# Loads paced by attention ticks, a machine model with DMA queue and clock, pair scores in segment 0, and filler matmuls in a fused attention and feed-forward block

## The chip, the cores and the metric

The kernel runs on one core of one Trainium2 chip. The metric is device microseconds (us) of one execution, the median of the runs of a kernel. Every run also has a state: fast, or slow when it is more than 1.5% above the fastest run of the same kernel. "Span" is the time from the first to the last instruction of the one profiled execution; it is about 2 us shorter than the device time. The engines are called TensorE (PE in the profile, its weight loads PEld), VectorE (DVE), ScalarE (ACT), GpSimd (POOL) and SyncE (SP; its DMA issues appear as SPq).

## The reference

It is one block on `x` of 2048 tokens by 640 features, in bf16: layer norm, attention with 32 heads of 20 features, an output projection with a residual, then a second layer norm and a feed-forward part with 1728 hidden features. The attention goes through four segments of 512 tokens. In each, a causal softmax inside the segment is mixed, through a gate, with a linear-attention memory of the earlier segments. Cut to what matters:

```python
h  = x + attn(layernorm(x), wq, wk, wv, wo, beta)
h2 = h + silu(layernorm(h) @ w1) @ w2

# attn, for each segment s of 4 (L = 512 tokens), each of H = 32 heads (Dh = 20):
p     = softmax(qs @ ks.T * Dh**-0.5 + causal_mask)
a_dot = p @ vs
a_mem = (phi(qs) @ M) / (phi(qs) @ z + 1e-6)       # phi(t) = t + 1 if t > 0 else exp(t)
o     = sigmoid(beta) * a_mem + (1 - sigmoid(beta)) * a_dot
M, z  = M + phi(ks).T @ vs, z + sum(phi(ks))
# out = concat(o) @ wo
```

## The kernel before

The Python that builds the kernel does not write instructions in a fixed order. It declares tasks (a matmul group, an exp, a DMA) with a priority, the engines that may run them, an estimated cost and the buffers they need. A list scheduler then plays the tasks through a small model of the machine and emits them in the order that came out. On the chip each engine runs its instructions in exactly that order, with semaphores between the engines. **The model's times never run anywhere, but they decide the order.** This is the part of it that the change touches:

```python
LAT = {PE: 0.125, AC: 0.145, DV: 0.03, PO: 0.07, SP: 0.0}
# ... in schedule(), for each engine that is free, the ready task of lowest priority number:
                        pr = t.prio
                        if e == PE and pemode[0] is not None and t.mode != pemode[0]:
                            pr += 0.02
# ... and then its cost; TensorE always at full speed:
                    if e == SP:
                        engfree[e] = st + 0.06            # SyncE is free again after 0.06 us
                        if t.mode == "tr":                # transposes: a queue of their own
                            b = max(st, xbar[0])
                            xbar[0] = b + t.bw
                            end = b + t.bw + cost
                        else:                             # all other transfers
                            b = max(st, dmaq[0])
                            dmaq[0] = b + t.bw
                            end = b + t.bw + cost
```

All loads come first, whole, on SyncE:

```python
    load_x(0, 1, -100)
    # ... x 1, 2, 3
    load_w("q", wraw[:, 0, :, :], cw(A_wq), -96, 3.4, [(sT0, ["q"])])
    load_w("k", wraw[:, 1, :, :], cw(A_wk), -95, 3.4, [(sT0, ["k"])])
    load_w("wv", wv_sb[:, :, :], cw(A_wv), -94, 3.4)
    # ... beta, x 4-7, wo, x 8-11
    load_w("w1", w1_sb[:, :, :], cw(B_w1), -87, 9.0)
    # ... x 12-15
    dma("w2a", [], [(W["w2"], [0])], lambda e: e.dma_start(out=w2_sb[:, 0:NF - 1, :], ...), -85, 9.0, lane=lane_w2)
    # ... w2b
```

The attention of a segment is eight "ticks" of four heads. A tick has three score tiles (PTA, PTB, PTE). Each takes four of the eight PSUM banks (`sc`), one bank a head; ScalarE then takes the exp, in halves or at once, and GpSimd the causal mask:

```python
            for pi, (pool, pt, js, width, cost) in enumerate((
                    ("PTA", PTA, [(0, 0)], 512, 0.225), ("PTB", PTB, [(1, 0), (3, 384)], 512, 0.23),
                    ("PTE", PTE, [(2, 0)], 256, 0.12))):
                sca = G.alloc("sc", 4)                    # all four score banks: the next tile has to wait
                # ...
                G.task(f"qk{k}{pi}", {PE: cost}, e_qk, [ra], [(sca, [0])], pr - 0.5, mode="r", reserve=[pta])
                halves = [(0, 2), (2, 2)] if width == 512 else [(0, 4)]
                # ... one exp for each half
            # evictions from PSUM may run on either engine:
            G.task(f"oe{k}", {AC: act_c(512) + 0.05, DV: dve_c(512)}, e_ot, ...)
```

The softmax here doesn't subtract the row's maximum and nothing guards it: scores larger than these inputs give would overflow.

Of the kernel before, what the change touches and what calls it, by code (L numbers as in the profile page):

```python
# [22 lines left out]
class _Op:  # L23
    __slots__ = ("eng", "fn", "seq", "waits", "need_inc", "lane", "cnt")

    def __init__(self, eng, fn, seq, lane=None):
        self.eng = eng
        self.fn = fn
        self.seq = seq
        self.waits = []  # L30
        self.need_inc = False
        self.lane = lane
        self.cnt = None

# [9 lines left out]
class Tracker:  # L44


    def __init__(self):
        self.ops = {e: [] for e in ENGS}
        self.K = {e: {} for e in ENGS}
        self.post = {}  # L50
        self.regions = {}
        self.lanes = []

# [23 lines left out]
    def add(self, eng, fn, reads=(), writes=(), order=(), lane=None):  # L77
# [6 lines left out]
        op = _Op(eng, fn, seq, lane=lane)  # L84
        if lane is not None:
            lane.n += 1
            prodkey, pseq = lane, lane.n
        else:
            prodkey, pseq = eng, seq
# [140 lines left out]
LAT = {PE: 0.125, AC: 0.145, DV: 0.03, PO: 0.07, SP: 0.0}  # L230


class Graph:
    def __init__(self, pools):
        self.pools = pools
        self.tasks = []
        self.turns = {}
        self.free_order = ("x", "ps", "ex", "th", "st", "xn", "pK", "rd")
# [42 lines left out]
    def schedule(self):  # L281
# [14 lines left out]
        xbar = [0.0]  # L296
# [48 lines left out]

        now = 0.0
# [5 lines left out]
        while left:  # L352
            progressed = True
            while progressed:
                progressed = False
                for e in ENGS:
# [3 lines left out]
                    for i in cand[e]:  # L360
# [3 lines left out]
                        pr = t.prio  # L364
                        if e == PE and pemode[0] is not None and t.mode != pemode[0]:
                            pr += 0.02
# [4 lines left out]
                        best = ((pr, t.idx), t)  # L371
                    if best is None:
# [14 lines left out]
                    if e == PE:  # L387
                        pemode[0] = t.mode
                    t.start, t.eng = st, e
                    if e == SP:  # L390
                        engfree[e] = st + 0.06
                        if t.mode == "tr":
                            b = max(st, xbar[0])
                            xbar[0] = b + t.bw
                            end = b + t.bw + cost
                        else:
                            b = max(st, dmaq[0])
                            dmaq[0] = b + t.bw
                            end = b + t.bw + cost
# [61 lines left out]

def build(nc, es, A_x, A_wq, A_wk, A_wv, A_wo, A_beta, B_x, B_w1, B_w2, out):
# [53 lines left out]
    mt = sb("mt", [128, 4, 96], F32)  # L516
    wraw = sT[:, :, :].rearrange("p f t -> p (f t)")[:, 0:2 * NC * D].rearrange("p (w c e) -> p w c e", w=2, c=NC)
# [14 lines left out]
    def act_c(n):  # L532
        return 0.00083333 * n + 0.075

    def dve_c(n):
        return n / 960.0 + 0.195
# [10 lines left out]
    def dma(name, reads, writes, fn, prio, bw, mode=None, lat=2.0, lane=None):  # L547
        ln = T.lane(name) if lane is None else lane

        def emit(eng):  # L550
            T.add(SP, lambda e: fn(e), reads=R(*reads), writes=R(*writes), lane=ln)
        return G.task(name, {SP: lat}, emit, reads, writes, prio, mode=mode, bw=bw)
# [9 lines left out]
    def load_x(b0, n, prio):  # L562
        dma(f"x{b0}", [], [(X[b], [0]) for b in range(b0, b0 + n)],
            lambda e: e.dma_start(out=x_tok[:, b0:b0 + n, :], in_=xv[:, b0:b0 + n, :]), prio, 0.68 * n)

    def load_w(k, dst, src, prio, bw, wr=None):
        dma("w_" + k, [], wr or [(W[k], [0])], lambda e: e.dma_start(out=dst, in_=src), prio, bw)

    cw = lambda w: w.rearrange("(c p) e -> p c e", p=128)
    load_x(0, 1, -100)  # L570
    load_x(1, 1, -99)
    load_x(2, 1, -98)
    load_x(3, 1, -97)
    load_w("q", wraw[:, 0, :, :], cw(A_wq), -96, 3.4, [(sT0, ["q"])])
    load_w("k", wraw[:, 1, :, :], cw(A_wk), -95, 3.4, [(sT0, ["k"])])
    load_w("wv", wv_sb[:, :, :], cw(A_wv), -94, 3.4)
    dma("beta", [], [(C, ["beta_bc"])],
        lambda e: e.dma_start(out=beta_bc[:, :],
                              in_=A_beta.rearrange("(o n) -> o n", o=1).to_broadcast([128, H])), -93, 0.3)
    load_x(4, 4, -90)  # L580
    load_w("wo", wo_sb[:, :, :], cw(A_wo), -89, 3.4)
    load_x(8, 4, -88)
    load_w("w1", w1_sb[:, :, :], cw(B_w1), -87, 9.0)
    load_x(12, 4, -86)
    lane_w2 = T.lane("w2")
    dma("w2a", [], [(W["w2"], [0])],
        lambda e: e.dma_start(out=w2_sb[:, 0:NF - 1, :], in_=cw(B_w2[0:(NF - 1) * 128, :])), -85, 9.0, lane=lane_w2)
    dma("w2b", [], [(W["w2"], [1])],
        lambda e: e.dma_start(out=w2_sb[0:64, NF - 1, :], in_=B_w2[(NF - 1) * 128:FF, :]), -84, 0.4, lane=lane_w2)  # L589
# [10 lines left out]
    def vx_alloc(s):  # L600
        VX[s] = G.alloc("Vx")
        return VX[s]

# [70 lines left out]
    rearr("wq", 0, wqr, -40)  # L674
    rearr("wk", 1, wkr, -39)
    WSUB = {"wq": list(range(5)), "wk": list(range(5)), "wv": [0], "wo": [0], "w1": [0], "w2": [0, 1]}


    def layer_norm(tag, b, xa, xsub, dstA, dst, i, prio):
        st = G.alloc("st")  # L680
        xn = G.alloc("xn")

# [9 lines left out]
        G.task(f"{tag}st{b}", {DV: 1.25}, e_stats, [(xa, xsub)], [(st, ["s0", "s1", "mv"])], prio)  # L692
# [9 lines left out]
        def e_apply(eng):  # L702
# [5 lines left out]
        G.task(f"{tag}ap{b}", {DV: 0.48}, e_apply, [(xa, xsub), (st, ["mv", "r"])], [(xn, [0])], prio)  # L708
        dma(f"{tag}tr{b}", [(xn, [0])], [(dstA, [i])],
            lambda e: e.dma_start_transpose(out=dst[:, :, 128 * i:128 * i + 128], in_=xn_rot[:, xn.slot, :]),  # L710
            prio, 0.9, mode="tr", lat=1.8)
# [8 lines left out]
    segs = {}  # L720

    def declare_front(s):

        k0 = 8 * s
        sg = segs[s] = {}
        xTa = G.alloc("xT")
        for i in range(4):
            layer_norm("n1_", 4 * s + i, X[4 * s + i], [0], xTa, xT, i, k0 - 5.0 + 0.6 * i if s else -30 + i)
        vx = vx_alloc(s)
        for i in range(4):  # L730
            ps = G.alloc("ps", 2)
            pr = k0 - 2.2 + 0.4 * i if s else -5 + i
# [24 lines left out]
        for c in range(5):  # L757
            for w in range(2):
                ps = G.alloc("ps", 1)
                pr = k0 - 1.2 + 0.65 * c + 0.3 * w if s else -10 + 0.5 * c + 0.2 * w + (0 if c < 2 else 8)  # L760
# [19 lines left out]
                if phi:  # L780
# [13 lines left out]
                    prp = k0 + 0.3 + 0.5 * c if w == 0 else k0 + 1.0 + 0.8 * c  # L794
                    G.task(f"ph{s}{c}{w}", {DV: 0.75}, e_phi, [(qk[c], [w]), (exa, [0])], [(pa, ["a"])], prp)
# [4 lines left out]
        pr = k0 + 2.6  # L800

        def virt(n, reads, o, i_):
            dma(f"vt{s}{n}", reads, [(qv, [n])], lambda e: e.dma_start(out=o, in_=i_), pr, 0.15, lane=lane_v)  # L803
# [8 lines left out]
    def declare_ticks(s):  # L812
# [3 lines left out]
        ot = G.alloc("otok")  # L816
        sg["ot"] = ot
        for g in range(NG):
# [7 lines left out]
            pts = []  # L826
            for pi, (pool, pt, js, width, cost) in enumerate((
                    ("PTA", PTA, [(0, 0)], 512, 0.225), ("PTB", PTB, [(1, 0), (3, 384)], 512, 0.23),
                    ("PTE", PTE, [(2, 0)], 256, 0.12))):
                sca = G.alloc("sc", 4)  # L830
                pta = G.alloc(pool)
                pts.append(pta)
                pr = k + (0.0, 0.35, 0.7)[pi]

                def e_qk(eng, sca=sca, js=js, qa=qa, ka=ka, ra=ra):
                    fns = []
                    for j, co in js:
                        n = L - 128 * j
                        for r in range(4):
                            fns.append(lambda e, j=j, co=co, n=n, r=r: e.matmul(  # L840
                                sc_all[:, 512 * r + co:512 * r + co + n],
                                lhsT=ka[32 * r:32 * r + DH, 128 * j:128 * j + 128],
                                rhs=qa[32 * r:32 * r + DH, 128 * j:L],
                                start=True, stop=True, tile_position=(32 * r, 0)))
                    T.run(PE, fns, R(ra), R((sca, [0])))
                G.task(f"qk{k}{pi}", {PE: cost}, e_qk, [ra], [(sca, [0])], pr - 0.5, mode="r", reserve=[pta])
                halves = [(0, 2), (2, 2)] if width == 512 else [(0, 4)]
# [307 lines left out]
```

## Time and profile before

| | before |
|---|---|
| device time, median of 2 runs | 447.04 us (446.94 to 447.15) |
| profiled span | 444.3 us |
| mean granted TensorE clock | 0.888 |
| TensorE busy / idle | 325.0 / 119.3 us |
| ScalarE, VectorE, GpSimd busy | 236.0, 205.1, 145.4 us |

The page of the kernel before, its parts 1 and 2. In part 2 each digit is one fortieth of the span (11.1 us), in tenths; PEclk is the granted clock of TensorE.

```profile
PE 325.0 (73%) x2616; PEld 160.0 (36%) x2616; DVE 205.1 (46%) x427; ACT 236.0 (53%) x304; POOL 145.4 (33%) x282
...
PE   0009858785569746865399999999977989665997
...
PEclk9999977987598955599599999999997999885999
```

No engine is full on average, and that average hides stages: three slices in which TensorE does nothing, a stretch in which it is about three quarters busy at a falling clock, a full stretch, and a tail with holes. I cut the span at five events: the first useful matmul, the last exp of segments 0, 1 and 3, and the end. The view of stretches of the kernel before; the columns are the stretch, its length, the busy time of PE, PEld, DVE, ACT and POOL with their instructions, the granted clock, the share of the DMA engines' time, and GB/s:

```profile
0.00:33.40 33.40, 0.00 (x0) 0.00 (x0) 8.65 (x25) 1.63 (x3) 11.47 (x47) 1.00 0.96 319
33.40:120.10 86.70, 63.11 (x496) 29.02 (x496) 47.01 (x121) 59.05 (x77) 34.65 (x72) 0.84 0.21 41
120.10:189.30 69.20, 50.53 (x452) 22.98 (x452) 26.84 (x57) 49.79 (x60) 29.96 (x49) 0.73 0.15 23
189.30:378.30 189.00, 163.48 (x1395) 83.24 (x1395) 98.54 (x182) 116.45 (x150) 64.07 (x103) 0.95 0.17 38
378.30:444.30 66.00, 47.85 (x276) 24.80 (x273) 24.11 (x43) 9.04 (x15) 5.29 (x11) 0.87 0.14 34
```

TensorE is idle for 33.4, 23.6, 18.7, 25.5 and 18.2 us in the five stretches (length less PE busy), and in segments 0 and 1 what it does runs at a clock of 0.84 and 0.73. The timeline of the kernel before says why the first stretch is empty; the columns are start, duration, engine and line, and, in brackets, the idle time before it and what ended it:

```profile
17.35 8.62 SPq L589 DMA_DIRECT2D w_sb<-in_B_w_dram  x1
26.02 10.47 SPq L710 DMA_TRANSPOSE xT<-xn_rot  x4
...
33.43 2.85 PE L738 MATMUL ps_gen<-wv_sb,xT 128*128 128x320 bf16 x10 [33.43 <-DMA xT<-xn_rot]
...
119.04 11.88 SPq L803 DMA_DIRECT2D QKV<-QK  x16
```

The first transpose of the normalised input, which every projection needs, is issued at 26.0 us, after all the loads, and lands at 33.4, behind the bytes still in flight. The last line shows the same at a smaller scale: 16 small copies hold SyncE for 11.9 us, and only then, at 131.0, can it issue the transposes for the output projection. The view of waits of TensorE in the kernel before (us in total, times, longest):

```profile
PE ps_gen L738 <- DMA xT<-xn_rot: 35.6, 2, 33.4
PE ps_sc L840 <- ACT PTB L851: 15.3, 13, 1.9
PE ps_gen L1060 <- DMA hT<-xn_rot: 12.7, 2, 8.8
```

So the big waits are the start, the score matmuls (L840) waiting until the exp has freed the one four-bank score buffer, and transposes of the tail.

### The profile page before, as it was taken

The page shows a single profiled execution, that of the slowest core. Times are in us where ns is not written, and L with a number is a line of the kernel's source. Part 1 is how long each engine was busy: PE and PEld are TensorE (multiplying, and loading weights), DVE is VectorE, ACT ScalarE, POOL GpSimd, SP SyncE. Part 2 cuts the span into 40 slices and gives each one's busy share as a digit, 9 for nine tenths or more (in the row PEclk, how much of TensorE's full clock was granted, in tenths as well). Part 3 has the DMA queues.
Part 4 walks back from the last instruction along what each step waited for, and adds up shares of the span by engine and source line. Part 5 has one row for each costly group of instructions (what it writes and reads, how often), then busy time and mean ns, then how long its engine had stood idle before and what let it go on. Part 6 is the DMA issues. An engine that isn't in the chain of part 4 may idle for free.

```text
span 444.3 us, 6635 instructions
## 1 busy us (share of the span) xinstructions
PE 325.0 (73%) x2616; PEld 160.0 (36%) x2616; DVE 205.1 (46%) x427; ACT 236.0 (53%) x304; POOL 145.4 (33%) x282
## 2 busy tenths in 40 slices
PE   0009858785569746865399999999977989665997
PEld 0005324332135322333144554455532445332444
DVE  6105735737125621575464256533763653271432
ACT  1004835987745978686065268767654875101420
POOL 9103535242322644554221032334442334120000
PEclk9999977987598955599599999999997999885999
DMA  8991331013034100044300310002321000221001
GB/s 268 349 343 30 55 74 37 12 38 71 12 50 46 25 0 1 12 77 94 77 1 1 75 45 1 1 15 60 74 56 21 2 15 16 68 52 30 1 15 44
DMA packets 51438, 25.17 MB, mean 57 GB/s; under 512 B 41488, under 2 KB 50128, under 8 KB 51408
## 3 DMA queue, kind: packets, MB, share of 16 engines
q1 hardware_dynamic: 51408, 24.76, 22.8%
q8 instruction: 20, 0.33, 0.3%
q14 instruction: 10, 0.08, 0.1%
HBM read 10.33 MB, written 2.62 MB: 29 GB/s over the span
## 4 chain that ended last, share of the span: by engine, by line
PE 53%; ACT 15%; SPq 14%; DVE 7%; DMA 6%; issue 3%; POOL 0%; POOLq 0%; ACTq 0%; DVEq 0%
PE ps_gen L1088 14%; PE ps_gen L1060 13%; PE ps_gen L766 8%; SPq L803 6%; PE ps_gen L1040 5%; ACT PTB L851 5%; PE ps_gen L738 4%; PE ps_sc L840 4%; ACT PTA L851 4%; PE ps_gen L877 2%; DMA xT<-xn_rot 2%; SPq L710 2%; SPq L589 2%; ACT PTE L851 2%; DMA hT<-xn_rot 2%
## 5 line engine op out<-in xcount | busy, mean ns | idle before, releaser
L1060 PE MATMUL ps_gen<-hT,w_sb 128*128 128x512 bf16 (+1 forms) x280 | 71.2, 401 | 15.1 <-DMA hT<-xn_rot 12.7
L851 ACT ACTIVATE PTB<-ps_sc 128x1024 bf16<-128x1024 f32 x64 | 62.0, 1025 | 24.9 <-PE ps_sc L840 24.8
L851 ACT ACTIVATE PTA<-ps_sc 128x1024 bf16<-128x1024 f32 x64 | 62.1, 1026 | 18.2 <-PE ps_sc L840 18.1
L1088 PE MATMUL ps_gen<-w_sb,sT 128*128 128x320 bf16 x448 | 69.6, 300 | 1.4 <-DVE on L946 0.7
L1067 ACT ACTIVATE th<-ps_gen 128x512 f32<-128x512 f32 (+1 forms) x56 | 33.4, 601 | 70.0 <-PE ps_gen L1060 69.0
L861 POOL TENSOR_SCALAR_AFFINE_SELECT PTB<-PTB 128x512 bf16<-128x512 bf16 x64 | 41.0, 641 | 74.4 <-ACT PTB L851 72.1
L1072 DVE SCALAR_TENSOR_TENSOR sT<-th,ps_gen 128x512 bf16<-128x512 f32 (+1 forms) x56 | 38.2, 687 | 52.3 <-ACT th L1067 51.9
L738 PE MATMUL ps_gen<-wv_sb,xT 128*128 128x320 bf16 x160 | 28.8, 340 | 35.8 <-DMA xT<-xn_rot 35.6
L1088 PEld LDWEIGHTS ps_gen<-w_sb,sT 128*128 128x128 bf16 x448 | 40.1, 97 | 26.5 <-issue 8.2
L1060 PEld LDWEIGHTS ps_gen<-hT,w_sb 128*128 128x128 bf16 (+1 forms) x280 | 26.5, 103 | 50.8 <-issue 21.8
L1040 PE MATMUL ps_gen<-wo_sb,oT 128*128 128x320 bf16 x160 | 29.2, 344 | 18.6 <-DVE on L946 8.9
L861 POOL TENSOR_SCALAR_AFFINE_SELECT PTA<-PTA 128x512 bf16<-128x512 bf16 x32 | 20.3, 634 | 63.2 <-ACT PTA L851 63.2
L851 ACT ACTIVATE PTE<-ps_sc 128x1024 bf16<-128x1024 f32 x32 | 32.7, 1023 | 11.9 <-PE ps_sc L840 11.9
L840 PE MATMUL ps_sc<-QK 20*128 20x512 bf16 (+3 forms) x320 | 23.4, 326 | 13.6 <-ACT PTB L851 8.0
L738 PEld LDWEIGHTS ps_gen<-wv_sb,xT 128*128 128x128 bf16 x160 | 16.6, 110 | 46.2 <-DMA xT<-xn_rot 35.8
L704 DVE TENSOR_SCALAR xn_rot<-x_tok,mvt,rst 128x640 bf16<-128x640 bf16 x32 | 15.4, 488 | 35.5 <-DMA xT<-xn_rot 25.7
L687 DVE BATCH_NORM_STATS2 stt<-x_tok 128x6 f32<-128x320 bf16 x64 | 28.0, 479 | 3.3 <-DMA x_tok<-in_A_x_dram 3.1
L766 PE MATMUL ps_gen<-xT,wqr 128*128 128x512 bf16 x100 | 27.1, 405 | 0.5 <-DVE on L946 0.4
L1040 PEld LDWEIGHTS ps_gen<-wo_sb,oT 128*128 128x128 bf16 x160 | 16.8, 110 | 29.5 <-issue 11.8
L766 PE MATMUL ps_gen<-xT,wkr 128*128 128x512 bf16 x100 | 26.3, 396 | 1.3 <-DVE x_tok L1048 0.9
L748 ACT ACTIVATE Vx<-ps_gen 128x640 bf16<-128x640 f32 x12 | 8.4, 703 | 34.2 <-PE ps_gen L738 34.0
L893 DVE TENSOR_SCALAR oTs<-ps_gen,lsc 128x512 bf16<-128x512 f32 x20 | 15.0, 748 | 23.4 <-PE ps_gen L877 23.1
(68 smaller groups left out, 404.5 us busy)
## 6 DMA issues: line engine op xcount, KB each, us to landing
out_dram<-x_tok SPq DMA_DIRECT2D x16, 160.0 KB, 1.8
w_sb<-in_B_w_dram SPq DMA_DIRECT2D x1, 2160.0 KB, 14.3
w_sb<-in_B_w_dram SPq DMA_DIRECT2D x1, 2080.0 KB, 17.0
x_tok<-in_A_x_dram SPq DMA_DIRECT2D x3, 640.0 KB, 11.1
QKV<-QK SPq DMA_DIRECT2D x16, 72.0 KB
sT<-in_A_wq_dram SPq DMA_DIRECT2D x1, 800.0 KB, 6.4
sT<-in_A_wk_dram SPq DMA_DIRECT2D x1, 800.0 KB, 8.1
wv_sb<-in_A_wv_dram SPq DMA_DIRECT2D x1, 800.0 KB, 9.7
```

Of the source, the lines that this page charges most:

```text
L687: T.add(DV, lambda e, hh=hh: e.bn_stats(out=stt[:, s, 6 * hh:6 * hh + 6], in_=xb[:, 320 * hh:320 * hh + 320]), reads=R((xa, xsub)), writes ...
L738: fns.append(lambda e, c=c, hh=hh: e.matmul(bank(ps, hh)[:, 0:320], lhsT=xT[:, c, 128 * i:128 * i + 128], rhs=wv_sb[:, c, 320 * hh:320 * h ...
L766: fns = [lambda e, kc=kc: e.matmul(bank(ps), lhsT=wt[:, kc, c, :], rhs=xT[:, kc, :], start=(kc == 0), stop=(kc == NC - 1)) for kc in range ...
L803: dma(f"vt{s}{n}", reads, [(qv, [n])], lambda e: e.dma_start(out=o, in_=i_), pr, 0.15, lane=lane_v)
L840: fns.append(lambda e, j=j, co=co, n=n, r=r: e.matmul(sc_all[:, 512 * r + co:512 * r + co + n], lhsT=ka[32 * r:32 * r + DH, 128 * j:128 * ...
L851: T.add(AC, lambda e: e.activation(out=pt[:, pta.slot, r0:r0 + nr, :], in_=sc3[:, r0:r0 + nr, 0:width], func=ACT.Exp, scale=SCALE), reads= ...
L861: fns.append(lambda e, v=v: e.affine_select(out=v, in_=v, pattern=[[0, 4], [1, 128]], compare_op=ALU.is_ge, fill=0.0, base=0, channel_mult ...
L1040: fns.append(lambda e, c=c, hh=hh: e.matmul(bank(ps, hh)[:, 0:320], lhsT=oT[:, c, 128 * i:128 * i + 128], rhs=wo_sb[:, c, 320 * hh:320 * h ...
L1060: fns = [lambda e, c=c: e.matmul(bank(ps)[0:fw, :], lhsT=w1_sb[:, c, 128 * f:128 * f + fw], rhs=hT[:, c, :], start=(c == 0), stop=(c == NC ...
L1067: T.add(AC, lambda e: e.activation(out=th[0:fw, tha.slot, :], in_=bank(ps)[0:fw, :], func=ACT.Tanh, scale=0.5), reads=R((ps, [0])), writes ...
L1072: T.add(DV, lambda e: e.scalar_tensor_tensor(out=sT[0:fw, f, :], in0=th[0:fw, tha.slot, :], scalar=1.0, in1=bank(ps)[0:fw, :], op0=ALU.add ...
L1088: fns.append(lambda e, f=f, fw=fw, hh=hh: e.matmul(bank(ps, hh)[:, 0:320], lhsT=sT[0:fw, f, 128 * i:128 * i + 128], rhs=w2_sb[0:fw, f, 320 ...
```

## The change

Its intent is to keep TensorE working, and at full clock, from start to end. It has six parts:

1. **Loads.** Only `x` 0 to 3, `wq`, `wk`, `beta` and `wv` stay at the start, `x` 4 to 7 follow the fourth normalised block, and the rest is paced by attention ticks, `w1` and `w2` in five pieces each.
2. **Model.** SyncE is charged 1.25, 0.72 or 0.45 us an issue, transposes share the one DMA queue with everything else, TensorE runs at half speed in the model after a window with little work, and the costs and latencies of VectorE and ScalarE are new.
3. **Priorities.** The constants formerly written in the code move into a table `P`, 22 of them with new values. They set, among others, that the second feed-forward layer comes later. The priorities of segment 0's first projections change too; they stay outside `P`.
4. **Eviction rule** ("flex"). ScalarE leaves an eviction to VectorE if the model says that VectorE is free within 1.042 us.
5. **Pair scores in segment 0.** A score tile is allocated as two pairs of banks, so the matmuls of one pair may run while the exp reads the other. The other segments keep four banks at once.
6. **Fillers.** Where the model finds TensorE without work and about to lose its clock, it inserts a matmul of zeros into a free PSUM bank.

The diff, cut to its core:

```diff
-LAT = {PE: 0.125, AC: 0.145, DV: 0.03, PO: 0.07, SP: 0.0}
+LAT = {PE: 0.125, AC: 0.16, DV: 0.14, PO: 0.09, SP: 0.0}
@@ schedule @@
+        WIN = 3.4133
+        def pe_rate(t):
+            w = int(t / WIN)
+            for v in range(max(rate), w):
+                rate[v + 1] = 1.0 if busy.get(v, 0.0) >= 0.39 * WIN else 0.5
+            return rate[w]
+        def fill_ok(t):
+            return t > self.fill_from and busy.get(int(t / WIN), 0.0) < 0.55 * WIN and t < self.fill_to
...
+                        if e == AC and DV in t.engs and engfree[DV] <= now + self.flex:
+                            continue
...
+                    if best is None and e == PE and self.filler is not None and fill_ok(now):
+                        # ... a task of 0.107 us that writes a free PSUM bank
...
-                        engfree[e] = st + 0.06
-                        if t.mode == "tr":
-                            ...
+                        engfree[e] = st + cost
+                        b = max(st + (0.9 if t.mode == "tr" else 0.3), dmaq[0])
+                        dmaq[0] = b + t.bw
+                        end = b + t.bw + 1.5
@@ build @@
+QUAD_SEGS = (1, 2, 3)
+P = {"ln1": -5.0, ..., "h2": 17.666, "h2s": 0.937, "h2q": 0.5, "flex": 1.042, "mode": 0.017, "h23": 0.392}
...
+    cost = {"tr": 1.25, "plain": 0.45, "sb": 0.72}[kind]
...
-    load_w("w1", w1_sb[:, :, :], cw(B_w1), -87, 9.0)
+    tick = lambda g: (f"nm{g}", lambda: [(segs[0]["ot"], [(0, g)])])
+    lnt = lambda i: (f"n1_ap{i}", lambda: [(segs[0]["xn"][i], [0])])
+    load_w("wv", wv_sb[:, :, :], cw(A_wv), -28.5, 2.7, [(W["wv"], [0])], after=lnt(1))
+    load_x(4, 4, -20, after=lnt(3))
+    load_w("wo", wo_sb[:, :, :], cw(A_wo), 0, 2.7, [(W["wo"], [0])], after=tick(0))
+    for c in range(NC):
+        load_w(f"w1_{c}", w1_sb[:, c, :], ..., 1 + c, 1.5, [(W["w1"], [c])], after=tick(1 + c))
+    # ... w2 in five pieces, x 8-11, x 12-15, after ticks 5 to 7
...
+    cst("zpad", DV, 0.3, lambda e: e.memset(zpad[:, :], 0.0), writes=["zpad"], prio=-80)
+    G.filler = lambda a: (lambda eng: T.run(
+        PE, [lambda e: e.matmul(bank(a)[:, 0:256], lhsT=zpad[:, 0:128], rhs=zpad[:, :], start=True, stop=True)],
+        R((C, ["zpad"])), R((a, [0]))))
...
-                sca = G.alloc("sc", 4)
+                quad = s in QUAD_SEGS
+                for r0, nr in ([(0, 4)] if quad else [(0, 2), (2, 2)]):
+                    sca = G.alloc("sc", nr)
...
-            pr = k0 + 14.7 + 0.8 * i
+            pr = k0 + P["h2"] + P["h2s"] * i + (P["h23"] if s == 2 else 0.0)
```

## The prediction

> **What bounds the kernel now.** Three things in turn, over a span of 444.3 us.
> (1) Start, 0 to 33.4 us: TensorE does nothing. The timeline shows SyncE issuing all 10.3 MB of loads first; the first xT transpose is issued at 26.0 and lands at 33.4 (35.6 us of TensorE idle "until DMA xT").
> (2) 34 to 220 us: ScalarE sets the pace and TensorE starves. The windows give TensorE 128 busy of 186 us and a clock of 0.90, 0.81, 0.70 in thirds. A steady tick (159 to 179 us) takes 6.85 us: 4.9 of exp, 0.69 of oTs eviction on ScalarE, the rest waits for scores that one four-bank buffer cannot hide. SyncE adds holes: 16 QKV copies hold it 11.9 us before the oT transposes (TensorE idle 4.4).
> (3) 220 to 330 us: TensorE-bound, 107 busy of 110 at clock 0.98 to 1.00. Then a tail from 383 to 444 with waits of 4.4 and 8.8 us for transposes at clock 0.68.
>
> **What the change does.** The new kernel's instruction order shows:
> - SyncE issues x, wq, wk, beta, then transposes; wv between them, all else later. wq and wk landed at 9.1 and 11.2; transposes queue behind them, so xT should be complete at 16 to 17 us. Saves about 17 us, all critical.
> - 31 QK, 12 Vx and 11 of 12 oTs evictions move from ScalarE to VectorE: ScalarE 236 to about 201 us, VectorE 205 to about 245.
> - Segment 0's pair scores hide the score wait (about 1 us a tick, eight ticks).
> - 134 filler matmuls of 256 columns, mostly in idle time, hold the clock near 1.0; five 512-column matmuls take 1.1 to 1.2 us warm and 2.2 to 2.3 cold here. The Trainium skill ("TensorE: Matmul & The Clock Gate", Part 1) says that idling halves the clock; the trace agrees. The 62 first fillers are not paced on the chip: they should end near 12 us and may let the clock fall again before xT arrives (2 to 3 us at most).
> - All 112 second-layer matmuls of segment 2 are kept back to fill the tail's waits (15.6 us of work).
>
> **Sum.** At full clock TensorE needs about 295 us: h1 60.5, h2 61, projections 43, V and wo 47, 32 ticks at 2.5, memory 6 (warm durations of the trace). First useful matmul at 14 to 16.5. Sixteen ticks at about 6.2 us put the last exp of segment 1 near 122 to 126 us (188 before). TensorE has then done about 105 us of its work; the other 190 at 96 to 97%, 4 us of ending and 4 to 8 of tail bubbles give a span of 325 to 337. I add some for in-order stalls.
>
> **Predicted: 342 us, 80% range 325 to 366.** Faster by over 2%: 0.98; within 2%: 0.01; slower: 0.01.
>
> **What would show it.** First useful matmul at 14 to 17 us; mean clock over 0.95 (0.888 before); ScalarE near 201 busy, VectorE near 245; segment 1's last exp by 130 us; a tail after the last exp of some 60 us with TensorE idle under 10; TensorE busy over 88% of the span.
>
> **What would make it wrong.** VectorE, in order, becoming the pacer (40 us more work; its evictions are 0.69 against 0.60 us); SyncE copies delaying segment 1's transposes; the static order stalling TensorE behind a late exp.

## The result, and the profile after

| | before | after |
|---|---|---|
| device time, median of 2 runs | 447.04 us | 348.26 us (348.15 to 348.37) |
| profiled span | 444.3 us | 346.4 us |
| mean granted clock | 0.888 | 0.990 |
| TensorE busy, fillers left out | 325.0 us | 298.3 us |
| fillers | none | 22.0 us |
| TensorE idle | 119.3 us | 26.1 us |

The ratio is 0.779 (95% interval 0.776 to 0.782). A ratio here is the mean time of one kernel's fast runs over the mean of the other's fast runs of the same rounds, so it is not quite the ratio of the medians in the tables. The result is correct against the reference, as it was in every run below.

The page of the kernel after, parts 1 and 2, and a group of part 5 from the view of groups (busy and mean ns, then the idle time before it):

```profile
PE 320.3 (92%) x2750; PEld 165.1 (48%) x2750; DVE 239.6 (69%) x482; ACT 203.8 (59%) x258; POOL 145.5 (42%) x282
...
PEclk9789999999999999999999999999999999999999
...
L669 PE MATMUL ps_gen<-zpad 128*128 128x256 bf16 x134 | 22.0, 298 | 2.3 <-DVE oTs L971 1.2 <-DVE zpad L667 1.1
```

The saving can be written as a sum of TensorE's time that closes exactly. Its useful busy time fell by 325.0 − 298.3 = 26.7 us: the same matmuls, fewer of them cold. Its idle time fell by 119.3 − 26.1 = 93.2 us. The fillers cost 22.0 us. So −26.7 − 93.2 + 22.0 = −97.9 us, which is 346.4 − 444.3. (Fillers and useful matmuls overlap for 4.6 us, which this counts as filler time; counted as useful work, it fell by 22.1 us. So read 26.7 as 22 to 27.)

Note what the 92% is not. The Trainium skill ("Perfetto Trace Analysis", Identifying the Most-Contended Engine) warns that the busy share of the matmuls is no good measure of the distance to the roofline. Here the trace agrees, for two reasons of its own: of the 320.3 us, 22.0 are zeros, and before, 325.0 busy held 22 to 27 us that the same matmuls no longer need after. Busy time of the two kernels is nearly equal and says nothing about which is better.

The view of stretches of the kernel after, cut at the same events (the first stretch ends with the first useful group of matmuls, not before it):

```profile
0.00:18.10 18.10, 11.87 (x72) 8.68 (x73) 9.78 (x32) 1.63 (x3) 13.49 (x59) 0.85 0.94 245
18.10:72.60 54.50, 51.55 (x450) 23.35 (x449) 39.07 (x81) 43.20 (x57) 26.10 (x44) 0.99 0.43 105
72.60:136.80 64.20, 58.63 (x561) 29.14 (x559) 58.00 (x126) 50.23 (x62) 34.50 (x64) 1.00 0.43 92
136.80:278.25 141.45, 135.85 (x1269) 68.94 (x1267) 101.56 (x193) 97.43 (x118) 66.03 (x105) 1.00 0.23 45
278.25:346.40 68.15, 62.41 (x405) 34.99 (x403) 31.20 (x53) 11.34 (x19) 5.35 (x11) 1.00 0.17 40
```

| stage | before | after | difference |
|---|---|---|---|
| to the first useful matmul | 33.4 | 15.5 | −17.9 |
| from there to the last exp of segment 0 | 86.7 | 57.1 | −29.6 |
| to the last exp of segment 1 | 69.2 | 64.2 | −5.0 |
| to the last exp of segment 3 | 189.0 | 141.5 | −47.5 |
| to the end | 66.0 | 68.2 | +2.2 |

Stages are not independent: a stage that ends sooner may simply have left work for the next. Segment 1 gained little, but it runs more matmuls than before (561 against 452, 38 of them fillers), and the tail contains all 112 second-layer matmuls of segment 2, of which 90 had been done before the tail until now (134 second-layer matmuls start there before, 224 after).

The timeline of the start of the kernel after:

```profile
5.70 4.07 SPq L780 DMA_TRANSPOSE xT<-xn_rot  x2
9.81 0.59 SPq L625 DMA_DIRECT2D wv_sb<-in_A_wv_dram  x1
10.45 2.93 SPq L780 DMA_TRANSPOSE xT<-xn_rot  x2
...
1.11 9.26 PE L669 MATMUL ps_gen<-zpad 128*128 128x256 bf16 x62 [1.11 <-DVE zpad L667]
15.49 2.83 PE L807 MATMUL ps_gen<-wv_sb,xT 128*128 128x320 bf16 x10 [5.13 <-DMA wv_sb<-in_A_wv_dram]
18.11 1.95 PE L835 MATMUL ps_gen<-xT,wqr 128*128 128x512 bf16 x5
...
20.98 1.52 PE L807 MATMUL ps_gen<-wv_sb,xT 128*128 128x320 bf16 x10
```

The first transpose is issued at 5.7 us in place of 26.0, and the first useful matmul starts at 15.5 in place of 33.4. The Trainium skill ("DMA: Bandwidth & Descriptors", Queues, rings and completion order) says that each DMA engine consumes the descriptors of one issuer in ring order. Both traces agree: a transpose that is issued behind or beside bulk loads takes 5.5 and 7.4 us (before) or 5.3 to 6.4 us (after) to land, and 2.6 to 2.7 us when nothing is ahead of it. So what counts is what stands ahead of the transposes in the queue, and that is what the change moved.

The start also shows a flaw. The 62 first fillers end at 10.4 us, then TensorE waits 5.1 us, and the first group of ten matmuls takes 2.83 us where the same group later takes 1.52. Three stretches of 3 us of the kernel after, with the clock in the third column from the right:

```profile
3.00:6.00 3.00, 3.00 (x16) 2.17 (x15) 2.81 (x10) 0.00 (x0) 2.60 (x11) 1.00 0.87 210
6.00:9.00 3.00, 3.00 (x29) 2.69 (x28) 2.37 (x8) 0.00 (x0) 2.80 (x9) 1.00 1.01 348
...
15.00:18.00 3.00, 2.50 (x10) 1.50 (x11) 0.00 (x0) 0.00 (x0) 1.74 (x12) 0.50 1.03 284
```

This is what the Trainium skill ("TensorE: Matmul & The Clock Gate", Part 1) describes: after an idle window of about 3.4 us the clock is half. Here 5.1 us of waiting gave 0.50.

The first two stretches hold nothing but fillers on TensorE, 16 and then 29 of them. So matmuls of zeros alone brought the clock up, near 6 us. They also show a trap: the clock column says 1.00 in both, although the matmuls of the first run at about half the pace. At the start of a run a 1.00 in this column is no evidence, and the mean of 0.990 leaves this cold stretch out.

For the tail, the timelines of both kernels, first before, then after:

```profile
387.18 8.46 PE L1040 MATMUL ps_gen<-wo_sb,oT 128*128 128x320 bf16 x40 [4.39 <-DMA oT<-otok]
...
404.45 7.25 PE L1060 MATMUL ps_gen<-hT,w_sb 128*128 128x512 bf16 x20 [8.81 <-DMA hT<-xn_rot]
```

```profile
285.42 8.09 PE L1166 MATMUL ps_gen<-w_sb,sT 128*128 128x320 bf16 x56 [0.64 <-DVE on L1024]
293.49 5.90 PE L1118 MATMUL ps_gen<-wo_sb,oT 128*128 128x320 bf16 x40
299.23 7.16 PE L1166 MATMUL ps_gen<-w_sb,sT 128*128 128x320 bf16 x50
```

Before, the output projection waited 4.4 us for one transpose and the next layer 8.8 us for another, and both then ran cold (8.46 us for 40 matmuls). Now second-layer matmuls of segment 2 (L1166) stand in both holes, and the same 40 matmuls take 5.90 us. This is what the Trainium skill ("Perfetto Trace Analysis", Optimization Strategy) advises for a kernel with several regimes, to interleave them: work of a dense stage was kept back for a stage that waits. TensorE is idle for 68.15 − 62.41 = 5.7 us of the tail, where it was 18.2.

The view of the chain that ended last sums up the change of regime, first before, then after:

```profile
PE 53%; ACT 15%; SPq 14%; DVE 7%; DMA 6%; issue 3%; POOL 0%; POOLq 0%; ACTq 0%; DVEq 0%
```

```profile
PE 67%; DVE 15%; ACT 7%; DMA 6%; issue 2%; SPq 1%; POOL 0%; ACTq 0%; DVEq 0%
```

SyncE's issues left the chain (14% to 1%), ScalarE halved, and VectorE doubled, as 54 evictions moved to it (in e5 below, where 39 go back, the shares are ACT 11% and DVE 10%): before, ScalarE did 31 of the Q and K projections, 12 of V and 12 of the attention outputs; after, it does one, of the last kind.

### The profile page after: what moved, and what is told of

The parts are those of the page before. It is cut to its first block, busy times and chain, and to the rows that moved or that the text cites. A ratio compares the mean times of both kernels' runs of the same rounds, so it can differ in the third digit from the quotient of the medians.

```text
span 346.4 us, 6896 instructions
## 1 busy us (share of the span) xinstructions
PE 320.3 (92%) x2750; PEld 165.1 (48%) x2750; DVE 239.6 (69%) x482; ACT 203.8 (59%) x258; POOL 145.5 (42%) x282
## 4 chain that ended last, share of the span: by engine, by line
PE 67%; DVE 15%; ACT 7%; DMA 6%; issue 2%; SPq 1%; POOL 0%; ACTq 0%; DVEq 0%
PE ps_gen L1166 17%; PE ps_gen L1138 16%; PE ps_gen L835 8%; PE ps_gen L807 7%; PE ps_sc L912 6%; PE ps_gen L1118 6%; PE ps_gen L955 4%; DVE QK L846 3%; ACT PTB L924 2%; ACT ex L851 2%; DMA xT<-xn_rot 2%; DVE on L1024 2%; DMA wv_sb<-in_A_wv_dram 2%; PE ps_gen L1057 2%; SPq L780 1%
## 5 line engine op out<-in xcount | busy, mean ns | idle before, releaser
L1166 PE MATMUL ps_gen<-w_sb,sT 128*128 128x320 bf16 (+1 forms) x448 | 68.6, 300 | 2.1 <-DVE on L1024 1.4
L1138 PE MATMUL ps_gen<-hT,w_sb 128*128 128x512 bf16 (+1 forms) x280 | 66.9, 380 | 2.4 <-DVE sT L1150 1.0
L1166 PEld LDWEIGHTS ps_gen<-w_sb,sT 128*128 128x128 bf16 (+1 forms) x448 | 40.1, 97 | 26.7 <-issue 8.0
L924 ACT ACTIVATE PTE<-ps_sc 128x1024 bf16<-128x1024 f32 (+1 forms) x40 | 33.4, 852 | 7.7 <-PE ps_sc L912 7.6
L846 DVE CAST QK<-ps_gen 128x512 bf16<-128x512 f32 x40 | 27.3, 684 | 9.9 <-ACT ex L851 8.4
L1176 DVE SCALAR_TENSOR_TENSOR x_tok<-ps_gen,x_tok 128x640 bf16<-128x640 f32 x16 | 13.2, 824 | 25.6 <-PE ps_gen L1166 25.6
L851 ACT ACTIVATE ex<-ps_gen 128x512 bf16<-128x512 f32 x30 | 17.7, 598 | 20.9 <-PE ps_gen L835 13.9
L971 DVE TENSOR_SCALAR oTs<-ps_gen,lsc 128x512 bf16<-128x512 f32 x31 | 23.0, 743 | 7.0 <-PE ps_gen L955 6.9
L1032 POOL TENSOR_TENSOR otok<-on 128x320 bf16<-128x320 bf16 x24 | 19.3, 804 | 18.6 <-DVE on L1024 15.0
L937 POOL TENSOR_SCALAR_AFFINE_SELECT PTE<-PTE 128x512 bf16<-128x512 bf16 x32 | 20.9, 652 | 10.4 <-ACT PTE L924 9.7
```

Of the source, the lines that this page charges most:

```text
L846: (lambda e: e.tensor_copy(out=o, in_=bank(ps)))
L851: T.add(AC, lambda e: e.activation(out=ex[:, exa.slot, :], in_=bank(ps), func=ACT.Exp), reads=R((ps, [0])), writes=R((exa, [0])))
L924: T.add(AC, lambda e: e.activation(out=pt[:, pta.slot, q0:q0 + nq, :], in_=sc3[:, b0:b0 + nq, 0:width], func=ACT.Exp, scale=SCALE), reads= ...
L937: fns.append(lambda e, v=v: e.affine_select(out=v, in_=v, pattern=[[0, 4], [1, 128]], compare_op=ALU.is_ge, fill=0.0, base=0, channel_mult ...
L1138: fns = [lambda e, c=c: e.matmul(bank(ps)[0:fw, :], lhsT=w1_sb[:, c, 128 * f:128 * f + fw], rhs=hT[:, c, :], start=(c == 0), stop=(c == NC ...
L1166: fns.append(lambda e, f=f, fw=fw, hh=hh: e.matmul(bank(ps, hh)[:, 0:320], lhsT=sT[0:fw, f, 128 * i:128 * i + 128], rhs=w2_sb[0:fw, f, 320 ...
```

## The experiments

The question after the result is which of the six parts earn the 98 us. My theory was that each part does in its own place what its name says. The rivals are that a part does little by itself, or that it works elsewhere. Each text names its own two theories, A and B, for its own part. Twelve kernels ran on three chips: the first four, the next four, the last four. Times are medians of all runs. The after kernel itself ran again; its ratio, **0.783 (0.780 to 0.786), is the control** for all the others. It comes from another chip than e1 to e8, which the ratio to the kernel before takes out only if chips differ by a factor.

| run | part undone (or done alone) | median us | ratio to before | above control |
|---|---|---|---|---|
| e9 | none (control) | 350.0 | 0.783 | |
| e1 | fillers | 355.8 | 0.796 | +1.3 points |
| e2 | paced loads | 369.5 | 0.826 | +4.3 |
| e3 | new priorities | 377.4 | 0.846 | +6.3 |
| e4 | pair scores in segment 0 | 367.8 | 0.824 | +4.1 |
| e5 | eviction rule | 351.9 | 0.788 | +0.5, within noise |
| e6 | machine model | 384.2 | 0.861 | +7.8 |
| e7 | pair scores in segment 1 too | 358.1 | 0.803 | +2.0 |
| e8 | start fillers made longer | 351.1 | 0.784 | none |
| e10 | `wv` first (faulty edit) | 358.0 | 0.800 | +1.7 |
| e11 | loads late but whole and unpaced | 349.7 | 0.783 | none |
| e12 | before, with paced loads alone | 415.3 | 0.928 | |

One point is 1% of the time before, 4.5 us.

**A correction to the texts for e3, e4 and e7.** In them I counted the ticks of the after kernel by its PTE exps. A tick in pairs has two of these and a tick in fours has one, so I was off by one: "65" is the seventh tick, not the eighth, and "128" is the fifteenth; the sixteenth ends at 136.8. The eighth tick's two PTE exps begin at 72.0 and 72.5 and end at 72.6 and 73.1: the cut at 72.6 in the views above is the end of the first, half a microsecond early. The comparisons below use the right ticks.

### e1_nofill: the fillers

The order is the same; the filler tasks emit nothing.

```diff
-    G.filler = lambda a: (lambda eng: T.run(PE, [lambda e: e.matmul(... zpad ...)], ...))
+    G.filler = lambda a: (lambda eng: None)
```

> The changed kernel with its 134 filler matmuls not issued; the order of everything else is the same. Theory A (fillers hold the clock): without them the granted clock falls to about 0.8 in the stretch of segments 0 and 1 (15 to 128 us) and the time rises by 8 us or more, to over 356. Theory B (the denser order holds the clock by itself, fillers are nearly free and nearly idle): mean clock stays over 0.95 after 20 us and the time moves by less than 4 us from 348.3.

Measured: 355.8 us (354.3 to 357.7), about 6 us above the control, with a mean clock of 0.971. The start is as before the edit: the first two groups take 2.83 and 1.97 us, as cold as with 62 fillers ahead of them. The difference lies in the middle. The view of stretches in segment 1, first of e1, then of the kernel after:

```profile
85.00:118.00 33.00, 24.91 (x217) 11.88 (x219) 27.68 (x65) 21.24 (x26) 18.52 (x35) 0.79 0.55 123
```

```profile
85.00:118.00 33.00, 28.50 (x287) 14.98 (x288) 30.51 (x70) 24.47 (x29) 19.93 (x38) 1.00 0.47 97
```

The clock falls to 0.79 there without fillers, and stays at 1.00 with them. Over the whole of segment 1 it falls to 0.89, less than theory A said (0.8). The rise of about 6 us lies between A (8 or more) and B (under 4). What follows: the fillers earn about 1.3 points, measured on another chip than the control (intervals 0.790 to 0.803 and 0.780 to 0.786), and all of it after the start. The 62 at the start bring nothing.

### e2_bulk: all loads first again

```diff
-    load_w("wv", ..., after=lnt(1)) ... load_x(12, 4, 10, after=tick(7))     # paced pieces
+    load_w("wv", ...); beta; load_x(4, 4, -90); load_w("wo", ...); load_x(8, 4, -88)
+    load_w("w1", ...); load_x(12, 4, -86); load_w("w2a", ...); load_w("w2b", ...)   # as before
```

> The changed kernel with all 10.3 MB of loads issued at the start as in the kernel before (same few large transfers, before the first transpose), all else as changed. Theory A (the start is wholly on the critical path): first useful matmul near 32 us instead of 15.5 and the time rises by 16 to 20 us, to 364 to 368. Theory B (the later stages have slack that absorbs a late start): it rises by less than 8 us.

Measured: 369.5 us. The first useful matmul comes at 33.7 us (15.5 after, 33.4 before), the eighth tick's last exps begin at 91.4 (72.0), the sixteenth's at 157.1 (135.8) and the last of all at 297.5 (277.2): 18 to 21 us late at every mark. Theory A was right: 19.5 us above the control. The start of the load queue lies fully on the critical path, and nothing later makes up for it.

### e3_oldprio: the old priority constants

```diff
-P = {"ln1": -5.0, "ln1s": 0.524, ..., "h1": 11.723, "h1s": 0.26, "th": -0.42, "h2": 17.666, "h2s": 0.937, ...}
+P = {"ln1": -5.0, "ln1s": 0.6, ..., "h1": 10.2, "h1s": 0.31, "th": -0.3, "h2": 14.7, "h2s": 0.8, ...}  # the literals of before
```

> The changed kernel with the scheduling priorities of the kernel before (27 retuned constants set back to the old literals), the VectorE rule for evictions, pairs, fillers, loads and models as changed. Theory A (the mechanisms bring the gain, the constants only fill the tail): 12 to 20 us slower, 360 to 368, most of it in the tail after the last exp. Theory B (the retuned order is the main gain): over 375, with TensorE idle in the middle too.

Measured: 377.4 us. (The text says 27 constants; its edit changes 22.) Theory A put the loss into the tail, where kept-back second-layer work would be missing. The tail is 66.7 us, no longer than with the new constants (68.2), though it holds fewer second-layer matmuls (161 against 224). The loss is in the middle: segment 0 ends at 78.7 (73.1), segment 1 at 148.3 (136.8), the last exp at 308.9 (278.3). So B was right: the constants are worth 6%, and what they earn lies in the order before the tail. **Keeping work back for the tail explains how the tail looks; the runs do not show that it is what the constants earn.**

### e4_quad0: four score banks in segment 0 too

```diff
-QUAD_SEGS = (1, 2, 3)
+QUAD_SEGS = (0, 1, 2, 3)
```

> The changed kernel with segment 0's scores computed four heads at a time on one four-bank buffer as in the other segments. Theory A (pairs hide the score wait, about 1 us a tick): 6 to 10 us slower, 354 to 358, and the eighth tick's last exp near 72 us instead of 65. Theory B (segment 0 is bound by TensorE work or VectorE evictions): under 3 us.

Measured: 367.8 us, some 18 us above the control. The eighth tick's last exp begins at 86.5 us (72.0 after). Both theories gave too small a size; A had the direction. The view of groups of ScalarE in segment 0 (18.5 to 86.5 us for e4, 18.1 to 72.6 for after), the exps of the first two tiles with the idle time before them; first e4, then after:

```profile
L924 ACT ACTIVATE PTB<-ps_sc 128x1024 bf16<-128x1024 f32 x16 | 15.5, 1025 | 6.3 <-PE ps_sc L912 6.3
L924 ACT ACTIVATE PTA<-ps_sc 128x1024 bf16<-128x1024 f32 x16 | 15.5, 1021 | 6.0 <-PE ps_sc L912 5.9
```

```profile
L924 ACT ACTIVATE PTB<-ps_sc 128x1024 bf16<-128x1024 f32 x16 | 15.8, 1032 | 1.7 <-PE ps_sc L912 1.5
L924 ACT ACTIVATE PTA<-ps_sc 128x1024 bf16<-128x1024 f32 x16 | 15.8, 1024 | 3.8 <-PE ps_sc L912 3.6
```

With the third tile the exps wait 14.1 us for scores in e4 and 6.0 us in the kernel after. So the hidden wait is real, 8 of the 14 us by which the segment ends later (87.5 against 73.1), and close to the "1 us a tick, eight ticks" of the prediction. The rest comes with the whole order, which changes with this one constant: ScalarE also waits 15.3 us before the 15 exps of phi that fall into the segment (11.0 us before 9 of them after), and the model puts 10.9 us of fillers into the segment (2.7 after). How the rest divides was not tested.

### e5_noflex: ScalarE may take evictions again

```diff
-     "h1s": 0.26, ..., "flex": 1.042, ...
+     "h1s": 0.26, ..., "flex": -1e9, ...
```

> The changed kernel with ScalarE allowed again to take any eviction that it is free for first (39 of about 54 return to it). Theory A (ScalarE paces segments 0 and 1, moving evictions off it matters): 5 to 15 us slower, 353 to 363, ScalarE near 228 us busy. Theory B (TensorE and the order pace it; the engine of an eviction hardly matters): under 3 us from the changed kernel's time.

Measured: 351.9 us (349.5 to 354.0). ScalarE is busy for 223.4 us in place of 203.8, VectorE for 215.2 in place of 239.6: 39 evictions went back. The time is within the noise of the control, as B said. In segment 1 VectorE is busy for 51.9 of 68.7 us (58.0 of 64.2 after), and the segment got no shorter. So VectorE alone does not set that segment's pace, and the large shift of evictions in the profile earns nothing measurable, at least for the 39 that went back.

### e6_oldmodel: the old machine model

The kernel after, but scheduled with the latencies and eviction costs of before, a TensorE always at full speed, 0.06 us an issue on SyncE, and a separate queue for transposes with the transfer times of before.

```diff
-LAT = {PE: 0.125, AC: 0.16, DV: 0.14, PO: 0.09, SP: 0.0}
+LAT = {PE: 0.125, AC: 0.145, DV: 0.03, PO: 0.07, SP: 0.0}
-                rate[v + 1] = 1.0 if busy.get(v, 0.0) >= 0.39 * WIN else 0.5
+                rate[v + 1] = 1.0
-                        engfree[e] = st + cost
+                        engfree[e] = st + 0.06      # and a queue of their own for transposes
```

> The changed kernel scheduled with the cost model of the kernel before (full clock always, SyncE instructions at 0.06 us, old latencies and eviction costs), all else as changed, the retuned constants too. Theory A (the order is only good where the model knows what SyncE and the clock cost): 10 to 30 us slower, with SyncE-released waits of several us on TensorE. Theory B (the retuned constants alone carry the order): under 6 us.

Measured: 384.2 us, 34 us above the control: theory A, and more than it said. It is the largest single loss. The view of waits of TensorE in e6:

```profile
PE ps_gen L1063 <- DMA phiKt<-phiK: 19.5, 4, 8.2
PE ps_gen L841 <- DMA xT<-xn_rot: 7.4, 1, 7.4
```

My reading is that the model believed that these transposes had arrived (its own times were not kept), and put matmuls that need them (L1063 is the memory, L841 a projection) ahead of work that was ready. An engine that runs in a fixed order then stands still: two lines, 26.9 us. In the kernel after the longest wait of TensorE for a transpose is 0.7 us. So the model as a whole is worth 34 us, and the two largest waits without it are for data that had not arrived. Three groups of constants were changed at once here (latencies and costs, the clock, SyncE with its queue); which of them counts most was not separated.

### e7_pair01: pair scores in segment 1 too

```diff
-QUAD_SEGS = (1, 2, 3)
+QUAD_SEGS = (2, 3)
```

> The changed kernel with pair scores in segment 1 as well. Theory A (the same score wait is there in segment 1): its last exp comes 5 us or more earlier than 128 and the time falls to 340 to 345. Theory B (by then TensorE's work is the limit, and the constants were tuned for the four-bank buffer there): no faster, 346 to 355.

Measured: 358.1 us, slower than the control by 2 points. In its profile segment 0 ends 4 us later than after (77.1), and segment 1, from there to its last exp at 134.0, takes 56.9 us (63.7 after): 7 us were gained. But the next tick's last exp begins only at 154.1, a gap of 21 us, where the kernel after has 11.5. At this border TensorE is busy for 13.1 of 13.5 us, between the last exp of segment 1 and the first of segment 2, with work that the faster segment had not done (461 matmuls in it, 561 after). The gain was given back at the border of the segments, which is theory B: the same device that saves 4 points in segment 0 costs 2 in segment 1.

### e8_longstart: fillers until the data arrives

```diff
+    # each of the fillers 15 to 62 is issued twice: 110 fillers at the start in place of 62
```

> The changed kernel with 48 more fillers at the start (110 for 62), so that they last until the first useful matmul at 15.5 us rather than ending at 10.4. Theory A (the clock falls in the 5 us gap and the first V and projection groups run cold, 2.83 and 1.95 us for 1.5 and 1.24): 1.5 to 2.5 us faster, 346 to 347. Theory B (the cold groups overlap waits that end later): within 0.5 us.

Measured: 351.1 us, and two of six runs were slow; the fast ones give 0.784, the control. The profiled run is a slow one, but what is read from it lies at its start, where its order is fixed. The timeline of the start of e8:

```profile
17.04 1.52 PE L815 MATMUL ps_gen<-wv_sb,xT 128*128 128x320 bf16 x10 [0.90 <-DMA wv_sb<-in_A_wv_dram]
21.09 1.91 PE L843 MATMUL ps_gen<-xT,wqr 128*128 128x512 bf16 x4 [2.54 <-DMA xT<-xn_rot]
```

The first group is now warm (1.52 us against 2.83), then waits 2.5 us for the rest of xT, and the next group is cold. In this profile the shorter group only made the wait longer. But here the last of the four transposes landed at 20.4 us, against 17.3 in the kernel after and 17.6 in the control's profile. The times agree with theory B, and yet a gain of 1.5 to 2.5 us (theory A) is no larger than what the intervals leave open (0.784, from 0.779 to 0.789). So e8 does not decide between them.

### e9_control: the kernel after, again

> The changed kernel itself, unedited, on the chip of the three runs beside it: the base for them. Theory A (runs differ by how the first loads happen to be served): its runs spread over 347 to 354 us and the spread is there at the first projection group already. Theory B (the changed kernel is steady): within 1 us of 348.3.

Measured: 350.0 us (348.3 to 354.0; the longest counts as slow), ratio 0.783. The spread is the one that theory A gave, but not where A put it: in the slow run that was profiled, the first projection group starts at 18.8 us, 0.7 later than in the kernel after. Two runs of the same kernel may therefore differ by about 1%, on one chip, in a kernel on one core. The profile fell on the slow run, so nothing is explained by it, except one caution: its clock is 0.91 between 45 and 85 us and 0.95 between 85 and 118 us, where the first profile of the kernel after has 1.00 in both. Part of what a single profile shows of the clock, in e1 too, is chance. The verdict on e1 rests on its ratio.

### e10_wvfirst: `wv` ahead of the transposes, a faulty experiment

```diff
+    wv = byname["w_wv"]
+    order.remove(wv)
+    order.insert(order.index(byname["n1_tr0"]), wv)      # and 90 fillers at the start
```

> The changed kernel with wv issued before the first xT transposes instead of between them, and 28 more fillers at the start (90 for 62); the order on the other engines is unchanged. Theory A (the last two transposes queue behind wv, so the first projection group at 18.1 us waits for bytes that are needed later): first V group near 13.5, first projection group near 16, 2 to 3 us faster than the control. Theory B (the three weight loads and the transposes share one bandwidth whatever their order): within 1 us.

Measured: 358.0 us, 8 us above the control, and it decides nothing. My edit kept the dependency that paces `wv`, and that one is written as a read of the second normalised block's buffer. Moved ahead of that block, the read became one that the block's write has to wait for. The timeline of VectorE shows it:

```profile
14.31 0.45 DVE L782 TENSOR_SCALAR xn_rot<-x_tok,mvt,rst 128x640 bf16<-128x640 bf16 x1 [7.64 <-DMA wv_sb<-in_A_wv_dram]
```

The second normalisation waits 7.6 us for a weight that it does not use. Whether an earlier `wv` would save the 2 us of cold matmuls at the start stays open.

### e11_late: late loads, whole and unpaced

All loads but those of the start are issued whole, in a row, right after the four transposes of segment 0.

```diff
-    for c in range(NC): load_w(f"w1_{c}", ..., after=tick(1 + c)) ... w2 in five pieces
+    load_w("wo", ..., -19, after=lnt(3)); load_x(8, 4, -18, after=lnt(3)); load_w("w1", ..., -17, after=lnt(3))
+    load_x(12, 4, -16, after=lnt(3)); load_w("w2a", ..., -15, after=lnt(3)); load_w("w2b", ..., -14, after=lnt(3))
```

> The changed kernel with the late loads neither split nor paced: the same few large transfers as in the kernel before, but issued after segment 0's four xT transposes. Theory A (pacing matters: copies and transposes of segment 0 queue behind 7 MB, about 22 us of loading): 8 to 20 us slower than the control. Theory B (it is enough to put the first transposes ahead of the bulk): within 4 us.

Measured: 349.7 us, ratio 0.783, the control. Theory B: splitting the loads and pacing them by ticks brings nothing that these runs can measure. What counts is that the first transposes are ahead of the bulk. This holds although the timeline shows SyncE held by the bulk, so that the first transpose for the memory comes at 30.55 us (24.05 after):

```profile
19.04 11.47 SPq L625 DMA_DIRECT2D w_sb<-in_B_w_dram  x2
```

### e12_paced_alone: the kernel before with paced loads only

```diff
 # in the kernel before: its loads replaced by the split and paced ones, nothing else
```

> The kernel before with only its loads changed, split and paced by ticks as in the changed kernel; its scheduler model, constants, pairs and evictions as before, no fillers. Theory A (the start's 17 us are worth as much without the rest): first useful matmul near 16 us and 15 to 19 us faster than the kernel before, 428 to 432. Theory B (the order of before gives part of it back in its ScalarE-paced segments): under 10 us faster.

Measured: 415.3 us (412.3 to 416.5), 32 us below before; theory A said 15 to 19. The first useful matmul comes at 16.2 us, 17 us sooner, and segment 0 ends 17 us sooner, at 103.1. By the end of segment 1 (184.6) 12 us of that are given back, and by the last exp (348.7) 30 us are gained; the tail is 66.0 us, as before. The view of stretches for segments 2 and 3 of e12, to be read beside the fourth line of before:

```profile
184.60:348.70 164.10, 141.79 (x1268) 73.43 (x1284) 86.14 (x167) 110.60 (x139) 64.63 (x105) 0.95 0.19 39
```

It is 164 us in place of 189 with fewer matmuls left to do there (1268 against 1395), since more were done in segment 1. So earlier loads did two things: they took 17 us off the start, as costed, and the order came out different (558 matmuls in segment 1 against 452, with one wait of 7.7 us for a transpose), which I take as the source of −12 and then +25 us. **A change of one part can reorder all engines, and here this side effect is as large as the effect that was intended.**

No version that was tried beats the kernel after.

## Why the prediction was right

The prediction of 342 us was 6 us low, inside the range of 325 to 366. Point by point:

- **Start: right.** First useful matmul predicted at 14 to 16.5 us, measured 15.5. All of it is critical: e2 shifts every later mark by 18 to 21 us, e12 gains 17 at once. xT is complete at 17.3 us in place of 16 to 17. The note that the first fillers end too early and let the clock fall came out: they end at 10.4 us (I said near 12), and the two first groups cost 2.83 + 1.95 us in place of 1.52 + 1.24, 2.0 us.
- **Clock: right.** Predicted over 0.95, measured 0.990 (0.976 to 0.990 in the control's fast runs). But the fillers, which I took for the means, earn only about 1.3 points (e1): without them the clock is still 0.971. That it is the denser order which holds it was theory B of e1; it fits, and was not tested alone.
- **TensorE's need at full clock: right.** Predicted 295 us, measured 298.3 without fillers. Busy share predicted over 88%, measured 92%, but only with the fillers in it; without them it is 86% (298.3 of 346.4).
- **Loads of ScalarE and VectorE: right in size, without effect.** Predicted 201 and 245 us, measured 203.8 and 239.6. Undone in e5, the move costs nothing measurable. In the prediction it stood among the things that the change does, and it earned nothing.
- **Pair scores in segment 0: right in mechanism.** About 8 us of exp's waits, as predicted; the order around it makes the effect 18 us (e4).
- **Tail: mechanism right, length wrong.** TensorE idle under 10 us: measured 5.7. "Some 60 us": measured 68.2, for it holds all 112 second-layer matmuls of segment 2. And e3 shows that the new constants do not earn their gain there.
- **Mis-sized term: "Sixteen ticks at about 6.2 us put the last exp of segment 1 near 122 to 126 us", "by 130".** Measured 136.8. Segment 0's eight ticks do take 6.1 us, (73.1 − 23.9) / 8 from its first exp on. Segment 1 takes 63.7 us, which is 8.0 us a tick. By then TensorE had done 103.9 us of useful work (the busy times of the first three stretches less 18.2 us of fillers), as the prediction's "about 105" has it, only 11 to 15 us later. The rest was right again: 194.4 us of useful work in the remaining 209.6 us, where I had summed 198 for the work and 8 to 12 for ending and bubbles.
- **Why the total held all the same.** The sum gave 325 to 337. I added "some for in-order stalls", and segment 1 used about that allowance. It was a guess of the right size, not a derivation.

What sets segment 1's 8 us is open. TensorE does 52.5 us of useful work there in 64.2, VectorE is 90% busy, less VectorE work (e5) does not shorten it, and more score buffers (e7) shorten it by 7 us but not the whole.

## What to carry to other kernels

Look first at what stands ahead of the first dependent transfer in the queue: moving the bulk behind it gave 17 us here, and pacing the bulk finely gave nothing more. Where a model decides a static order, keep the model honest about the machine (34 us here for all of it), and look first at the times at which data arrives, for which the two largest waits of e6 speak; filler matmuls and moved evictions are small change beside it (6 us and nothing). And since an edit may reorder every engine, judge parts by undoing them: here the six single undoings sum to 24.3 points where the whole is 21.7, paced loads are worth 4.3 points undone and 7.2 done alone, and the same trick (pair scores) gains in one segment and loses in the next.

## What the Trainium skill lacked or had wrong

- "TensorE: Matmul & The Clock Gate", Part 1, says that for modelling the ramp penalty is under 1% of a typical kernel span. That holds for one warm-up at the start. In the kernel before, where the clock was lost again and again, the useful matmuls took 22 to 27 us longer than after, 5 to 6% of 444.3. The same page describes such oscillation in its section on it; the remark about modelling does not point there.
- The same page does not say whether matmuls of zeros count as activity for the clock gate. They do: with nothing else on TensorE, 16 of them ran between 3 and 6 us and 29 between 6 and 9, and with 110 of them ahead the first useful group was warm (1.52 us in e8, 2.83 in e1 without any).
- "DMA: Bandwidth & Descriptors" gives what an issue costs only as cycle counts of earlier generations, in a passage on trn3, and no time measured for transfers like those of this kernel. With no bulk load under way a transpose of 128 by 640 inside SBUF holds SyncE for 1.2 to 1.3 us, one of 16 small copies for 0.74 us (11.88 us / 16).
- The same page has no figure for an issue that is held while bulk loads are under way. Here single issues took long among bulk loads: one of 80 KB held SyncE for 8.62 us before, two in a row for 11.47 us in e11, where a weight load issued early takes 0.43 to 0.59 us. The runs do not show the mechanism.
